# Gated channel mixing: the end of the kernel by batch pairs, its weights by way of DRAM, its gates without GpSimd

## The chip, the cores and the metric

One core of one Trainium2 chip runs the whole program. The metric is the device time of one execution in microseconds; a kernel's number is the median over its runs. A profile is one execution taken by the hardware profiler; in it TensorE is PE, VectorE is DVE, ScalarE is ACT, GpSimd is POOL and SyncE, which issues the DMAs, is SP.

## The reference

All tensors are float32, with 4 batches (B), 12 heads of 64, 448 positions (S) and 768 channels (D); the weights come as float64.

```
scores = q k^T / sqrt(64) - log(S);  x = sigmoid(scores) v        # heads joined: (4, 448, 768)
u = x + (x^T U V)^T                                              # U: 448 x 32, V: 32 x 448
y = u + relu(u w_ch1) w_ch2                                      # 768 -> 3072 -> 768
gate[:, s] = sigmoid(sum over k in 0..4 of conv_w[k] * y[:, s - 4 + k])     # per channel, zero ahead of s = 0
out = (gate * (y w_val)) w_out                                   # both weights 768 x 768
```

## The kernel before, in words

Channels lie on the 128 partitions, positions along the free dimension: `xs` holds x, then u, y and at last z = gate times value, as 6 channel blocks by 4 batches, each with four zeros ahead of its 448 positions (`x_of(b, m)` is one 128x448 block of it without the zeros). Every product with a weight is made of three passes of reduced precision (`mm3`, lines 175 to 177): high part by high part, high by low, low by high. So each operand is a pair of tiles, a rounded high part (ACT) and the rest, its low part (a subtraction). Operands lie in a pool of 32 slots (`operand`).

A weight comes in halves of 128x384 numbers as float64 bits (`load_half`, on SP's queue, three halves ahead) and is unpacked by four operations (`unpack`, lines 83 to 88), rounded by ACT (line 73) and subtracted by DVE (line 75) into a buffer of the pool `w` (`prep_half`). What `later=True` or `deferred` marks is put back until the next `flush`, which `product` and `ch2` call first, so that an engine's in-order queue does not wait there.

Stages, in the order in which the code is written (it is the order on each engine's queue; there is no other scheduler):

1. Attention by pairs of heads, woven with the mixing by U and V and the splitting of u. The first weights are unpacked beside it.
2. Twelve channel groups. A group has two chunks of 128 hidden channels: for each chunk and batch one `ch1` product (18 matmuls, relu and its low part), then for each batch and channel block one `ch2` (12 matmuls) whose result DVE adds to `xs`. Beside them stand 8 calls of `prep_half` a group, for the next group's weights.
3. In the last group every `ch2` is followed by `y_split`: high part on ACT, low part on POOL.
4. 24 value products `val(b, m)`, block by block over all four batches, with the value weights unpacked beside them; each is multiplied by its gate into z (line 432). The gate of a block takes five taps (`gate_steps`): three scalings on ACT (line 404), two additions on POOL (lines 410 and 414), two fused multiply-adds on DVE (line 417), a sigmoid on ACT (line 426). `before(i)` and `after(i)` spread these steps over the products around the i-th.
5. `z_split` for z of the first two batches beside the last four value products, of the others at the first two output products (lines 73 and 77).
6. 24 output products `fin` (block by block, all batches), each copied by ACT (line 441) and stored by SP (lines 619 and 621), with the output weights unpacked beside them.

Products go round through eight PSUM banks (`bank`).

Of the kernel before, what the change touches and what calls it, by code (L numbers as in the profile page):

```python
# [8 lines left out]
F32 = mybir.dt.float32  # L9
# [20 lines left out]
HQ = DM // 2  # L30
NP = B * H // 2
OPS = 32
WS = 5
LAG = 2
EARLY = 3

# [2 lines left out]
def tile_kernel(  # L39
# [82 lines left out]
    sources += [wval_in[m] for m in range(KC)] + [wout_in[m] for m in range(KC)]  # L122
    pools = {}
    wraw = {}
    wt = {}
    ready = set()
    at = {"load": 0, "prep": 0}

    def load_half():
        i = at["load"]  # L130
        if i >= 2 * len(sources):
            return
        n, half = divmod(i, 2)
        if i < EARLY:
            r = scratch(f"raw{i}")[:, :2 * HQ].bitcast(I64)
        else:
            r = pools["raw"].tile([P, HQ], I64, tag="raw", name=f"raw{i}")[:, :]
        nc.sync.dma_start(r, sources[n][:, half * HQ:(half + 1) * HQ])
        wraw[i] = words(r)
        at["load"] += 1  # L140

    def prep_half():
        i = at["prep"]
        if i >= 2 * len(sources):
            return
        flush()
        n, half = divmod(i, 2)
        if i < EARLY:
# [7 lines left out]
        wt.setdefault(n, []).append(t)  # L156
        unpack(wraw.pop(i), a, x)

        def high():
            split(f32(x), t[:, 0], t[:, 1], later=True)  # L160
            deferred.append(lambda: ready.add(i))

        deferred.append(high)
        at["prep"] += 1
# [3 lines left out]
    def weight(n):  # L168
        while not {2 * n, 2 * n + 1} <= ready:
            flush()  # L170
        return wt[n]

    def mm3(ps, w, k, x, start, stop):
        wk = w[k // 3][:, :, (k % 3) * P:(k % 3 + 1) * P]
# [205 lines left out]
    def ch2(g, b, m):  # L380
# [5 lines left out]
        y = x_of(b, m)  # L386
        nc.vector.tensor_add(y, ps[:, :S], y)  # L387

    def y_split(b, m):
        y = x_of(b, m)  # L390
        t = operand(f"y{b}_{m}")
        nc.scalar.activation(t[:, 0], y, AF.Copy)  # L392
        nc.gpsimd.tensor_sub(t[:, 1], y, f32(t[:, 0]))  # L393
        ys[b, m] = t

    def gate_steps(b, m):

        t = []
        y = xs[:, m, b]
        z = x_of(b, m)  # L400
        tap = lambda k: f32(cw[:, m * TAPS + k:m * TAPS + k + 1])

        def scaled(dst, k):
            nc.scalar.activation(dst, y[:, k:k + S], AF.Copy, scale=tap(k))

        def first():
            t.append(operand(f"g{b}_{m}", F32))
            scaled(t[0][:, 0], 0)
            scaled(t[0][:, 1], 1)
            nc.gpsimd.tensor_add(t[0][:, 0], t[0][:, 0], t[0][:, 1])  # L410

        def second():
            scaled(t[0][:, 1], 2)
            nc.gpsimd.tensor_add(t[0][:, 0], t[0][:, 0], t[0][:, 1])  # L414

        def fused(dst, k):
            nc.vector.scalar_tensor_tensor(
                dst, y[:, k:k + S], tap(k), t[0][:, 0], op0=ALU.mult, op1=ALU.add
            )

        return (
            first,
            second,
            lambda: fused(t[0][:, 0], 3),
            lambda: fused(z, 4),
            lambda: nc.scalar.activation(z, z, AF.Sigmoid),
        )

    def val(w, b, m):
        ps = product(f"val{b}_{m}", w, lambda k: ys[b, k])  # L430
        z = x_of(b, m)
        nc.vector.tensor_mul(z, ps, z)

    def z_split(b, m):
        t = operand(f"z{b}_{m}")
        split(x_of(b, m), t[:, 0], t[:, 1])
        zs[b, m] = t

    def fin(w, b, m, o):
# [83 lines left out]
    def main_phase(tail):  # L523
# [27 lines left out]
        ch1(0, B - 1)  # L551
        ch1(1, B - 1)

        todo = [(b, m) for m in range(KC) for b in range(B)]
        gates = [gate_steps(b, m) for b, m in todo]

        def gate(i, k):
            if 0 <= i < len(gates):
                gates[i][k]()

        def before(i):
            gate(i, 4)
            gate(i + 1, 2)

        def after(i):
            gate(i + 1, 3)
            gate(i + 2, 1)
            gate(i + 3, 0)

        for g in range(NG):  # L570
            n = 2 * G * g
            last = g == NG - 1
            if g == 0:
                flush()
            if g:
                for i in range(G):
                    for b in range(B):
                        ch1(g * G + i, b)
                        if i * B + b < 6:
                            prep_half()  # L580
                    wt.pop(n + i)
            for b in range(B):
                for m in range(KC):
                    ch2(g, b, m)
                    if last:
                        y_split(b, m)
                        if b == B - 1 and m in (2, 3, 4):
                            i = m - 5
                            before(i)
                            after(i)  # L590
                if g == 0 or last or b % 2 == 0:
# [5 lines left out]
        for i, (b, m) in enumerate(todo):  # L597
            before(i)
            val(weight(n + m), b, m)
            after(i)  # L600
            if m < KC - 1 and b in (0, 2):
                prep_half()
            if m == KC - 1:
                for k in range(3):
                    z_split(b // 2, 3 * (b % 2) + k)
        n += KC
        for m in range(KC):
            for p in range(2):
                o = operand(f"o{p}_{m}", F32)
                for j in range(2):  # L610
                    b = 2 * p + j
                    fin(weight(n + m), b, m, o[:, j])
                    if m == 0 and b < 2:
                        for k in range(KC):
                            z_split(b + 2, k)
                    if b >= 2:
                        prep_half()
                    if m == KC - 1 and p == 1:
                        nc.sync.dma_start(out[m, :, b], o[:, j])
                if m < KC - 1 or p == 0:  # L620
                    nc.sync.dma_start(out[m, :, 2 * p:2 * p + 2], o)

    with tc.manual_schedule():
        mixc = pool(ctx, "mixc", 1)
# [11 lines left out]
        next(work)  # L636
        att.close()
        end = scope()
        pools["w"] = pool(end, "w", 2 * WS)
        banks.append(pool(end, "ps_m", 4, space=PSUM))  # L640
        for _ in work:
            pass
# [43 lines left out]
```

## Time and profile before

| | |
|---|---|
| median of 3 runs | 1093.49 us (1092.12 to 1095.51) |
| the profiled execution | 1092.42 us, of which the span from the first to the last instruction is 1090.6 us |
| busy, share of the span | PE 1060.4 us (97%), DVE 683.1 (63%), ACT 330.8 (30%), POOL 91.9 (8%) |
| granted PE clock, mean | 0.989 of full |
| DMA | 70.64 MB, mean 65 GB/s |

Busy times are those of the engine's instructions, laid over each other only once. A clock of 1.00 is 2.4 GHz and one of 0.50 is 1.2 GHz.

### The profile page before, as it was taken

To read this page: it belongs to the slowest core of one execution; us is meant where nothing else is said; L and a number is where in the kernel's file an instruction comes from. 1 tells how busy PE (TensorE), PEld (TensorE's weight loads), DVE (VectorE), ACT (ScalarE), POOL (GpSimd) and SP (SyncE) were. 2 spreads that over 40 slices of the span, in tenths; PEclk is the share of its full clock that TensorE was granted. 3 is DMA by queue.
4 is the path that set the end of the run, shared out by engine and by line. 5 is a ranking of instruction groups with operands and counts; after the bars stand their busy time and mean duration, and the time that the engine had idled before them with its cause. 6 is when DMAs were issued, how large, how long until landed. Compare 5 with 4: busy or idle time off the path is not lost.

```text
span 1090.6 us, 13524 instructions
## 1 busy us (share of the span) xinstructions
PE 1060.4 (97%) x5464; PEld 901.5 (83%) x5464; DVE 683.1 (63%) x1247; ACT 330.8 (30%) x565; POOL 91.9 (8%) x77
## 2 busy tenths in 40 slices
PE   8999999999999999999999999999999999975998
PEld 3444446899999999999999999999999999964997
DVE  4454657786666666666566666666656788889510
ACT  5677776302010111111010202020111345557221
POOL 0000000000000000000000000000000485553000
PEclk9999999999999999999999999999999999995999
DMA  6333332213121211212121313121212212110311
GB/s 164 102 103 86 92 104 84 64 53 102 29 73 29 74 44 58 59 44 73 29 73 29 87 29 87 29 73 29 73 44 58 59 30 58 45 44 19 122 68 68
DMA packets 28303, 70.64 MB, mean 65 GB/s; under 512 B 3520, under 2 KB 7216, under 8 KB 28240
## 3 DMA queue, kind: packets, MB, share of 16 engines
q1 hardware_dynamic: 28160, 69.66, 22.5%
q8 instruction: 43, 0.70, 0.3%
q14 instruction: 20, 0.16, 0.1%
q10 hardware_dynamic: 80, 0.11, 0.0%
HBM read 64.26 MB, written 5.51 MB: 64 GB/s over the span
## 4 chain that ended last, share of the span: by engine, by line
PE 88%; POOL 5%; issue 3%; DVE 2%; ACT 0%; DMA 0%; SPq 0%; POOLq 0%; ACTq 0%
PE ch L175 21%; PE ch L177 21%; PE ch L176 21%; PE av L250 7%; PE sc L229 6%; PE fin L176 3%; PE fin L177 3%; PE fin L175 3%; POOL g L414 2%; POOL g L410 2%; PE tr L309 1%; PE pp L323 1%; PE h L345 1%; POOL y L393 1%; DVE z L77 0%
## 5 line engine op out<-in xcount | busy, mean ns | idle before, releaser
L387 DVE TENSOR_TENSOR xs<-ch,xs 128x448 f32<-128x448 f32 x288 | 175.8, 622 | 101.8 <-PE ch L177 101.7
L73 ACT ACTIVATE w<-x 128x384 fp32r<-128x384 f32 x120 | 63.0, 525 | 499.9 <-DVE x L88 496.4
L175 PE MATMUL ch<-u,w 128*128 128x448 f32 x576 | 210.9, 366 | 0.0
L175 PE MATMUL ch<-h,w 128*128 128x448 f32 x576 | 210.6, 366 | 0.0
L176 PE MATMUL ch<-h,w 128*128 128x448 f32 x576 | 210.6, 366 | 0.0
L177 PE MATMUL ch<-h,w 128*128 128x448 f32 x576 | 210.5, 366 | 0.0
L176 PE MATMUL ch<-u,w 128*128 128x448 f32 x576 | 210.5, 365 | 0.0
L177 PE MATMUL ch<-u,w 128*128 128x448 f32 x576 | 210.5, 365 | 0.0
L375 DVE SCALAR_TENSOR_TENSOR h<-ch,h 128x448 fp32r<-128x448 f32 x96 | 59.9, 624 | 133.2 <-ACT h L374 133.2
L175 PEld LDWEIGHTS ch<-u,w 128*128 128x128 f32 x576 | 108.3, 188 | 9.7 <-issue 1.3
L177 PEld LDWEIGHTS ch<-h,w 128*128 128x128 f32 x576 | 108.3, 188 | 8.4
L177 PEld LDWEIGHTS ch<-u,w 128*128 128x128 f32 x576 | 108.3, 188 | 8.4
L175 PEld LDWEIGHTS ch<-h,w 128*128 128x128 f32 x576 | 108.3, 188 | 8.4
L176 PEld LDWEIGHTS ch<-h,w 128*128 128x128 f32 x576 | 108.3, 188 | 8.4
L176 PEld LDWEIGHTS ch<-u,w 128*128 128x128 f32 x576 | 108.4, 188 | 8.3
L393 POOL TENSOR_TENSOR y<-xs,y 128x448 fp32r<-128x448 f32 x24 | 29.0, 1223 | 863.8 <-ACT y L392 863.4
L237 ACT ACTIVATE a<-sc,bias 112x896 f32<-112x896 f32 x96 | 91.5, 1002 | 24.3 <-PE sc L229 23.9
L75 DVE TENSOR_TENSOR w<-x,w 128x384 fp32r<-128x384 f32 x120 | 67.2, 560 | 30.6 <-ACT w L73 29.0
L374 ACT ACTIVATE h<-ch 128x448 fp32r<-128x448 f32 x96 | 51.1, 533 | 109.4 <-PE ch L177 109.3
L250 PE MATMUL av<-a,vr 112*64 112x448 f32 x384 | 82.8, 552 | 0.0
L229 PE MATMUL sc<-ks 64*112 64x448 f32 x576 | 73.4, 387 | 5.1 <-ACT ks L214 5.1
L229 PEld LDWEIGHTS sc<-ks 64*112 64x112 f32 x576 | 48.0, 176 | 30.5 <-ACT a L237 9.4
(75 smaller groups left out, 1183.1 us busy)
## 6 DMA issues: line engine op xcount, KB each, us to landing
raw<-in_w SPq DMA_DIRECT2D x96, 384.0 KB, 3.1
kq<-in_kq SPq DMA_DIRECT2D x47, 224.0 KB, 3.8
vr<-in_va SPq DMA_DIRECT2D x24, 224.0 KB, 2.6
out_t<-o SPq DMA_DIRECT2D x11, 448.0 KB, 2.5
raw<-in_wval SPq DMA_DIRECT2D x12, 384.0 KB, 3.1
raw<-in_wout SPq DMA_DIRECT2D x12, 384.0 KB, 3.2
out_t<-o SPq DMA_DIRECT2D x2, 224.0 KB, 1.9
vraw<-in_v SPq DMA_DIRECT2D x3, 112.0 KB, 3.7
```

The lines of the kernel that those rows point to most:

```text
L73: nc.scalar.activation(hi, raw, AF.Copy)
L75: deferred.append(lambda: nc.vector.tensor_sub(lo, raw, f32(hi)))
L175: mm(ps, wk[:, 0], x[:, 0], start=start, stop=False)
L176: mm(ps, wk[:, 0], x[:, 1], start=False, stop=False)
L177: mm(ps, wk[:, 1], x[:, 0], start=False, stop=stop)
L229: mm(ps[:SC, h, :S], ks[r, tk, 0, c * SC:(c + 1) * SC], ks[r, tq, 1], start=t == 0, stop=t == 2,)
L237: nc.scalar.activation(a[:SC], ps[:SC, :, :S], AF.Sigmoid, bias=bias[:SC], scale=1.0 / math.sqrt(D))
L250: mm(ps[D * h:D * h + D, :S], vr[:, h, c], a[:SC, h], start=c == 0, stop=c == NSC - 1,)
L374: nc.scalar.activation(t[:, 0], ps, AF.Relu)
L375: nc.vector.scalar_tensor_tensor(t[:, 1], ps, 0.0, f32(t[:, 0]), op0=ALU.max, op1=ALU.subtract)
L387: nc.vector.tensor_add(y, ps[:, :S], y)
L393: nc.gpsimd.tensor_sub(t[:, 1], y, f32(t[:, 0]))
```

## The change

Value and output weights (24 halves, numbers 96 to 119) are unpacked inside the channel groups, in a written-out sequence `order` ("c" is a half of a channel group's weight, "s" one of these), at 10 or 11 `prep_half` a group. When such a half is done it is written to DRAM (`stash`) and its buffer is free again. In the end it is read back (`fetch`) once for each pair of batches, without unpacking. The pool `w` has 11 buffers where it had 10.

The last group and everything behind it run by pairs of batches: ch1 and ch2 of batches 0 and 1, then of 2 and 3; value products of the first pair, of the second; output products of the first pair, of the second. Gates are made for two batches in one operation of 128x896: one scaling on ACT, four fused multiply-adds on DVE, one sigmoid on ACT; two of the twelve beside the second pair's ch1, the others beside the value products. The low part of y is subtracted on DVE. z is split one block per product: the first pair's beside the second pair's value products, the second pair's beside the first pair's output products. One of `unpack`'s operations is ACT's instead of DVE's.

```diff
-WS = 5
+WS = 11
@@ unpack
-        nc.vector.tensor_scalar(a, f32(high), 2.0 ** -112, None, op0=ALU.mult)
+        nc.scalar.activation(a, f32(high), AF.Copy, scale=2.0 ** -112)
@@ the sequence of halves
+    plan("c" * 9 + "cccscs")
+    for g in range(1, NG - 1):
+        plan("ccccccss" + ("ccs" if g < 3 else "cc"))
+    plan("ccc")
@@ prep_half
+        def done(t):
+            ready.add(i)
+            if i >= 4 * NF:
+                stash[i] = pools["stash"].tile([P, 2, HQ], F32, tag="stash", name=f"s{i}")
+                nc.sync.dma_start(stash[i][:, :, :], f32(t))
+    def fetch(n, p):
+        fetched[n, p] = ts = []
+        for half in range(2):
+            t = pools["w"].tile([P, 2, HQ], F32R, tag="w", name=f"f{n}_{p}_{half}")[:, :, :]
+            nc.sync.dma_start(f32(t), stash[2 * n + half][:, :, :])
+            ts.append(t)
@@ y_split
-        nc.gpsimd.tensor_sub(t[:, 1], y, f32(t[:, 0]))
+        lows[b, m] = lambda: nc.vector.tensor_sub(t[:, 1], y, f32(t[:, 0]))
@@ gate_steps(bs, m), y(k) = xs[:, m, both batches, k:k + S]
+            nc.scalar.activation(t[0], y(0), AF.Copy, scale=tap(0))
+        def add(k):
+            nc.vector.scalar_tensor_tensor(
+                y(k) if k == PAD else t[0], y(k), tap(k), t[0], op0=ALU.mult, op1=ALU.add
+            )
@@ the value products
+        for v, (p, m, b) in enumerate(todo):
+            later.append((v // 2, val(fetched[n + m, p], b, m)))
+            settle_values(1)
+            gate_half()
+            y_low()
+            if p:
+                z_split(*unsplit.pop(0))
+            if v % 2:
+                fetch_next()
```

What this makes of DVE's queue in the middle of the value products. Before (val1_2 is the value product of batch 1 and block 2, g2_2 the gate of batch 2 and block 2, the last number is the program's):

```order
L417 SCALAR_TENSOR_TENSOR xs_61<-xs_61,cw_62,g1_2_7751 128x448
L83 TENSOR_SCALAR a107_7825<-raw107_7624 128x384
L84 TENSOR_SCALAR x107_7826<-raw107_7624 128x384
L85 SCALAR_TENSOR_TENSOR x107_7826<-a107_7825,x107_7826 128x384
L88 SCALAR_TENSOR_TENSOR x107_7826<-raw107_7624,x107_7826 128x384
L417 SCALAR_TENSOR_TENSOR g2_2_7790<-xs_61,cw_62,g2_2_7790 128x448
L432 TENSOR_TENSOR xs_61<-val1_2_7836,xs_61 128x448
L417 SCALAR_TENSOR_TENSOR xs_61<-xs_61,cw_62,g2_2_7790 128x448
L417 SCALAR_TENSOR_TENSOR g3_2_7820<-xs_61,cw_62,g3_2_7820 128x448
L75 TENSOR_TENSOR w107_7824<-x107_7826,w107_7824 128x384
```

Of the change, at two value products of the first pair (g2_0 is now the gate of batches 2 and 3 in block 0):

```order
L467 TENSOR_TENSOR xs_61<-val1_3_7931,xs_61 128x448
L447 SCALAR_TENSOR_TENSOR g2_0_7900<-xs_61,cw_62,g2_0_7900 128x896 x2
L427 TENSOR_TENSOR y3_2_7718<-xs_61,y3_2_7718 128x448
L467 TENSOR_TENSOR xs_61<-val0_4_7961,xs_61 128x448
L447 SCALAR_TENSOR_TENSOR g2_0_7900<-xs_61,cw_62,g2_0_7900 128x896
L447 SCALAR_TENSOR_TENSOR xs_61<-xs_61,cw_62,g2_0_7900 128x2x448
L427 TENSOR_TENSOR y3_3_7728<-xs_61,y3_3_7728 128x448
```

The unpacking is gone from here, the two fused steps of a block have become four of double length per pair, and a low part of y stands after each half gate; the multiplication by gate comes one product late.

DVE's queue at the turn to the output products, before (z0_3 is the split z of batch 0 and block 3):

```order
L417 SCALAR_TENSOR_TENSOR g3_5_8234<-xs_61,cw_62,g3_5_8234 128x448
L432 TENSOR_TENSOR xs_61<-val2_5_8283,xs_61 128x448
L417 SCALAR_TENSOR_TENSOR xs_61<-xs_61,cw_62,g3_5_8234 128x448
L77 TENSOR_TENSOR z1_0_8304<-xs_61,z1_0_8304 128x448
L77 TENSOR_TENSOR z1_1_8307<-xs_61,z1_1_8307 128x448
L77 TENSOR_TENSOR z1_2_8310<-xs_61,z1_2_8310 128x448
L432 TENSOR_TENSOR xs_61<-val3_5_8314,xs_61 128x448
L77 TENSOR_TENSOR z1_3_8334<-xs_61,z1_3_8334 128x448
```

And of the change:

```order
L467 TENSOR_TENSOR xs_61<-val3_3_8261,xs_61 128x448
L75 TENSOR_TENSOR z0_4_8311<-xs_61,z0_4_8311 128x448
L467 TENSOR_TENSOR xs_61<-val2_4_8291,xs_61 128x448
L75 TENSOR_TENSOR z1_4_8334<-xs_61,z1_4_8334 128x448
L467 TENSOR_TENSOR xs_61<-val3_4_8314,xs_61 128x448
L75 TENSOR_TENSOR z0_5_8361<-xs_61,z0_5_8361 128x448
L467 TENSOR_TENSOR xs_61<-val2_5_8341,xs_61 128x448
L75 TENSOR_TENSOR z1_5_8384<-xs_61,z1_5_8384 128x448
L467 TENSOR_TENSOR xs_61<-val3_5_8364,xs_61 128x448
L75 TENSOR_TENSOR z2_0_8413<-xs_61,z2_0_8413 128x448
```

The last gate steps have moved ahead of these rows, and the splits of z are spread, one by one, between the multiplications.

## Rows read from the trace of the kernel before

**Rows 1.** The summary page: span, busy time, and the granted clock in 40 slices.
```profile
span 1090.6 us, 13524 instructions
PE 1060.4 (97%) x5464; PEld 901.5 (83%) x5464; DVE 683.1 (63%) x1247; ACT 330.8 (30%) x565; POOL 91.9 (8%) x77
...
PEclk9999999999999999999999999999999999995999
```

**Rows 2.** Stretches: length, busy PE, PEld, DVE, ACT, POOL (instructions); clock, DMA share, GB/s.
```profile
350.00:880.00 530.00, 530.00 (x2616) 491.86 (x2616) 337.23 (x657) 82.10 (x163) 16.99 (x15) 1.00 0.20 55
884.87:974.37 89.50, 88.18 (x433) 80.78 (x431) 75.53 (x105) 50.64 (x91) 56.18 (x44) 1.00 0.16 45
974.37:993.35 18.98, 0.17 (x1) 0.00 (x0) 16.79 (x24) 11.25 (x22) 11.57 (x10) 0.64 0.14 42
993.35:1003.54 10.19, 8.74 (x21) 6.80 (x22) 10.19 (x17) 6.73 (x15) 2.22 (x2) 0.50 0.00 1
1003.54:1086.65 83.11, 83.11 (x412) 77.10 (x410) 24.15 (x52) 21.32 (x44) 0.00 (x0) 1.00 0.24 83
```

**Rows 3.** PE in order of time, from the last value matmul on: start, duration.
```profile
974.17 0.37 PE L177 MATMUL val<-y,w 128*128 128x448 f32 x1
993.35 0.74 PE L175 MATMUL fin<-z,w 128*128 128x448 f32 x1 [18.81 <-ACT z L73]
...
1003.54 0.38 PE L175 MATMUL fin<-z,w 128*128 128x448 f32 x1
...
1086.65 0.37 PE L177 MATMUL fin<-z,w 128*128 128x448 f32 x1
```

**Rows 4.** Waits from 884 to 994 us: total, times, longest.
```profile
POOL g L414 <- ACT g L404: 36.4, 20, 2.9
...
PE fin L175 <- ACT z L73: 18.8, 1, 18.8
```

**Rows 5.** The gates' tiles: duration ns least, median, most; first and last start.
```profile
L404 ACT ACTIVATE g<-xs,cw x72: 651/655/673, 887.8 to 994.6; 128x448 f32<-128x448 f32 x72
L410 POOL TENSOR_TENSOR g<-g x24: 1117/1220/1552, 889.6 to 992.9; 128x448 f32<-128x448 f32 x24
...
L417 DVE SCALAR_TENSOR_TENSOR g<-xs,cw,g x24: 674/682/1567, 893.1 to 1000.2; 128x448 f32<-128x448 f32 x24
L417 DVE SCALAR_TENSOR_TENSOR xs<-xs,cw,g x24: 670/680/1383, 894.7 to 1001.3; 128x448 f32<-128x448 f32 x24
```

**Rows 6.** DVE's groups from 884 to 1004 us: busy us, mean ns, idle before.
```profile
L417 DVE SCALAR_TENSOR_TENSOR g<-xs,cw,g 128x448 f32<-128x448 f32 x24 | 25.9, 1080 | 15.2 <-POOL g L414 15.2
L417 DVE SCALAR_TENSOR_TENSOR xs<-xs,cw,g 128x448 f32<-128x448 f32 x24 | 20.5, 856 | 0.1
L432 DVE TENSOR_TENSOR xs<-val,xs 128x448 f32<-128x448 f32 x24 | 14.7, 614 | 0.0
L83 DVE TENSOR_SCALAR a<-raw 128x384 f32<-128x384 f32 x11 | 13.8, 1255 | 0.0
```

**Rows 7.** DVE's unpacking, groups from 0 to 880 us.
```profile
L88 DVE SCALAR_TENSOR_TENSOR x<-raw,x 128x384 uint32<-128x384 uint32 x101 | 57.2, 567 | 3.5
L75 DVE TENSOR_TENSOR w<-x,w 128x384 fp32r<-128x384 f32 x101 | 55.7, 552 | 2.9 <-ACT w L73 1.4
...
L83 DVE TENSOR_SCALAR a<-raw 128x384 f32<-128x384 f32 x99 | 36.8, 372 | 0.0
```

**Rows 8.** The one DVE operation with two inputs of 128x896, in attention.
```profile
L210 DVE TENSOR_TENSOR ks<-kq,ks x23: 1091/1092/1094, 8.8 to 167.0; 128x896 fp32r<-128x896 f32 x23
```

**Rows 9.** ACT's copies (line 73), and DVE in time at the z splits.
```profile
L73 ACT ACTIVATE w<-x x120: 514/525/529, 174.1 to 1054.7; 128x384 fp32r<-128x384 f32 x120
...
L73 ACT ACTIVATE z<-xs x24: 559/564/573, 992.7 to 1010.0; 128x448 fp32r<-128x448 f32 x24
...
1004.07 8.11 DVE L77 TENSOR_TENSOR z<-xs,z 128x448 fp32r<-128x448 f32 x15
```

**Rows 10.** DMA issues: count, KB each, median us to landing.
```profile
raw<-in_w SPq DMA_DIRECT2D x96, 384.0 KB, 3.1
```

More of the change, by code (lines that the diff above doesn't have):

```diff
@@ L125, in tile_kernel @@
     wt = {}
+    stash = {}
+    fetched = {}
     ready = set()
@@ L419, in fused, with rest @@
             )
+        def rest():
+            y_low(*[(b, m) for b in bs])
+            add(3)
+            add(4)
         return (
             first,
[L423 to L426, printed above, removed]
+            lambda: (add(1), add(2)),
+            rest,
+            lambda: nc.scalar.activation(y(PAD), y(PAD), AF.Sigmoid),
         )
     def val(w, b, m):
+        y_low(*[(b, k) for k in range(KC)])
@@ L552, in main_phase @@
         ch1(1, B - 1)
[L554 to L570, printed above, removed]
+        for g in range(NG - 1):
             n = 2 * G * g
-            last = g == NG - 1
             if g == 0:
@@ L584, in main_phase @@
                     ch2(g, b, m)
[L585 to L591, printed above, removed]
+                    if m == KC // 2 - 1 and b % 2 and g == 0:
+                        prep_half()
+                if g == 0 or b % 2 == 0 or (b == 1 and g < 3):
                     prep_half()
@@ L594, in main_phase @@
                 wt.pop(n + G + i)
-        n = 2 * G * NG
[L597 to L605, printed above, removed]
+        halves = [range(h, h + B // 2) for h in range(0, B, B // 2)]
+        gates = [gate_steps(bs, m) for bs in halves for m in range(KC)]
@@ new lines, in main_phase, with gate_half @@
+        open_at = [0]
+        finished = []
+        def gate_half():
+            i, k = divmod(open_at[0], 2)
+            if i >= len(gates):
+                return
+            open_at[0] += 1
+            gates[i][1 + k]()
+            if k:
+                if i + 2 < len(gates):
+                    gates[i + 2][0]()
+                deferred.append(lambda: (gates[i][3](), finished.append(i)))
+        n = 2 * G * NG
+        g = NG - 1
+        fetches = [(n + q * KC + m, p) for q in range(2) for p in range(2) for m in range(KC)]
@@ new lines, in fetch_next @@
+        def fetch_next():
+            if fetches:
+                fetch(*fetches.pop(0))
+        for p, bs in enumerate(halves):
+            for i in range(G):
+                for b in bs:
+                    ch1(g * G + i, b)
+                    if p == 0:
+                        prep_half()
+                    else:
+                        y_low()
+                        y_low()
+                        gate_half()
+            if p:
+                for _ in range(3):
+                    fetch_next()
+            for b in bs:
+                for m in range(KC):
+                    ch2(g, b, m)
+                    y_split(b, m)
+                    if p == 0 and m % 2:
+                        y_low()
+            if p == 0:
+                flush(every=True)
+                gates[0][0]()
+                gates[1][0]()
@@ L606, in main_phase @@
         n += KC
-        for m in range(KC):
-            for p in range(2):
+        for p, bs in enumerate(halves):
+            for m in range(KC):
                 o = operand(f"o{p}_{m}", F32)
[L610 to L618, printed above, removed]
+                end = p and m == KC - 1
+                for j, b in enumerate(bs):
+                    fin(fetched[n + m, p], b, m, o[:, j])
+                    settle_values(0)
+                    if unsplit:
+                        z_split(*unsplit.pop(0))
+                    if end:
```

69 lines of the change are left out of this document (41 added, 28 removed).

## The prediction

> **What bounds the kernel now.** I read the summary first: TensorE (PE) is busy 97% of a span of 1090.6 us, and the granted clock is below full in one slice only, close to the end [rows 1]. So everything that is not PE at its pace is to be looked for there. The table by stretches then shows the middle of the program (350 to 880 us): PE busy all the time at full clock [rows 2]. In the stretch of the 432 matmuls of the value products it is busy 88.18 of 89.50 us; then comes a stretch of 18.98 us in which PE does nothing; then 10.19 us at half clock (1.2 instead of 2.4 GHz), for 21 matmuls; and from 1003.54 us on full clock again, without a gap [rows 2].
>
> The pace of PE when nothing holds it: from 1003.54 to 1086.65 us there are 410 steps from one matmul's start to the next one's (432 output matmuls less the first 21 and less one), so 83.11/410 = 0.2027 us a step [rows 2, 3]. One product of 18 matmuls is 3.65 us, a value stage or an output stage of 24 products 87.57 us.
>
> Why PE stands still: its longest wait, 18.8 us, is that of the first output matmul for the high half of z on ScalarE (ACT) [rows 4]. z is gate times value, and the gates were late. The list of waits says where they were made: GpSimd (POOL) waits for ACT's scaled taps and the others for POOL in turn [rows 4], the first of POOL's two additions per gate alone takes 1.2 us, the second goes the same way [rows 5], and the 24 gates stretch from 887.8 us (the first scaled tap) to 1001.3 (the start of the last step on VectorE) [rows 5]: 4.7 us per gate against 3.65 us per value product. PE runs ahead until the PSUM banks are full (PE then loses 1.9 us inside the stage), and at the turn to the output stage all that lag is paid at once, with the clock on top: it is at half rate after the standstill.
>
> **The change, part by part.**
>
> *What can be won.* The three losses, each against the pace of 0.2027 us: value stage 974.37 - 884.87 - 87.57 = 1.93 us (974.37 is the last value matmul's start, 974.17, and a step); standstill 993.35 - 974.37 = 18.98 us; half clock 10.19 - 21 x 0.2027 = 5.93 us [rows 2, 3]. Sum 26.84 us. PE has the same matmuls before and after, so this is the most that the end can give, and what is left to ask is whether the new order feeds PE without a wait.
>
> *Gating on VectorE (DVE).* Per channel block and batch pair there are now one ACT scaling, four fused multiply-adds of 128x896 on DVE and one sigmoid on ACT, 12 times. The trace has no fused operation of that length. Undisturbed, the 128x448 one takes 0.67 us (its minimum; the median is 0.68) [rows 5]. A two-operand instruction goes from 0.614 us at 448 columns [rows 6] to 1.092 us at 896 [rows 8], so 0.48 us for 448 more. I take 0.67 + 0.48 = 1.15 us. Bounds: below, 1.09 us, the row of 896 itself; above, twice the mean that the fused operations had beside POOL, 2 x (1.080 + 0.856)/2 = 1.94 us [rows 6].
>
> *Is DVE fast enough?* Two value products are 7.30 us of PE. In that time DVE has one gate (4 x 1.15 = 4.60), two multiplications of value by gate (2 x 0.614) [rows 6] and two low halves, of y in the first pair's products, of z in the second's (at most 2 x 0.614; fifteen of them in a row took 8.11 us, 0.54 each [rows 9]). That is 7.06 us, or 97%. Tight, but two of the twelve gates are made earlier, beside the second pair's ch1 products, the other ten beside the first twenty value products; the last four products have no gate and leave 4 x (3.65 - 1.23) = 9.7 us for catching up. DVE falls behind the end of the stage only if a fused operation takes over 1.15 + (10 x 0.24 + 9.7)/40 = 1.45 us.
>
> The 1.15 us hang on what slowed DVE before. The row: the same multiplication of 128x384 took 372 ns on average before 880 us [rows 7] and 1255 ns in the stretch in which POOL works [rows 6]. The Trainium skill, page "SBUF — State Buffer", section "Who interferes with whom", says that VectorE and GpSimd share one pair of SBUF ports, and that a VectorE instruction in a two-port mode or with two SBUF inputs and a GpSimd instruction block each other. By that rule the fused operation without POOL takes its undisturbed time and the sum is the one below; without it the 1.94 us stay and the time is that of the second rival. The trace agrees so far as it goes: the fused operations' minimum of 670 ns stands beside maxima of 1383 and 1567 [rows 5].
>
> *ACT in that stage.* Per two products a scaling and a sigmoid of 896, and two copies of 0.56 us [rows 9]. From 384 to 448 columns such a copy goes from 525 to 564 ns [rows 9], so 448 more are worth some 0.27 us, and at most a whole scaling of 448 once more, 0.66 us [rows 5]. The four sum to 2.9 us, at most 3.7, of 7.30. Not a bound.
>
> *The turn to the outputs.* Before, z was split after the last value products, three blocks at a time in front of the queue. Now the first pair's twelve z splits stand beside the second pair's value products, and the second pair's beside the first pair's output products: when the first output matmul comes up, all of its z but the last ones are done for many microseconds. I charge nothing; the cover is the second pair's 12 products (43.8 us). The same holds for y: the first pair's y is split during its ch2 and the second pair's ch1, the second pair's ch2 (144 matmuls, 29 us, in which DVE has 12 additions of the length of a multiplication by gate) follows before anybody needs it.
>
> *Channel groups: 24 unpackings of a half weight come into them*, one after each of the 8 ch1 products and two or three in ch2. One of the four unpacking operations goes from DVE to ACT. A half costs DVE 0.372 for the multiplication that stays, twice 0.567 and 0.552, 2.06 us instead of 2.43 [rows 7], and ACT 0.525 twice (an estimate for the scaling from the copy of the same shape [rows 9]). With the relu's low half a ch1 product takes 2.7 of 3.65 us of DVE and 1.6 of ACT. PE has eight banks of results in hand there. I charge 0; if the cover were gone, each would cost PE about the added ACT operation, 24 x 0.525 = 12 us. Before the groups, in the attention part, ACT gets six operations of at most 0.58 us among sigmoids with which PE never waits for it; below 3 us, I take 0.
>
> *DRAM.* 24 writes and 48 reads of 384 KB on SP's queue. A load of that size took 3.1 us from issue to landing [rows 10], so a weight of two halves 6.2 us even if one followed the other, and one is asked for per 7.30 us. Three weights are fetched before the value stage starts, during the second pair's ch2; each next one waits on SP only for a buffer whose last reader is several products back. What stands behind a fetch in SP's queue is the next fetch and, in the output stage, the output stores, which nobody waits for until the end. DMA engines were busy 24% at 83 GB/s in the output stage [rows 2]; two halves per 7.30 us are 108 GB/s, in place of the loads there, which keeps it below half. Charge 0. The queue also holds 24 stores that wait for a low half on DVE, with the next raw load behind them; the raw loads are three halves ahead, 11 us in ch1, against a landing of 3.1 us.
>
> *The end* (last copy, last stores) is the same: 0.
>
> **Sum.** Span 1090.6 - 26.84 = 1063.8 us; around the span there are 1092.42 - 1090.6 = 1.8 us, so 1065.6 us for the profiled execution. The median of the runs, 1093.49, is 1.07 us above that execution, so 1093.49 - 26.84 = 1066.65. I put 0.35 us on it for new hand-overs and forecast **1067 us**, 2.4% less. A change of 0.3% (3.3 us) is about what a measurement of this kernel can tell from none.
>
> **Rivals.**
>
> 1. *Part of the wait stays at the turn* (chance 0.09). DVE at 97% may run late by some microseconds, if a fused operation is not 1.15 but, say, 1.57 us (40 x 0.12 = 5 us over what the slack takes), or if the in-order queues wait for each other as long. Then the first output matmul waits 5 us, and the half clock comes back as it did after the standstill, another 5.9 us [rows 2]: 1066.65 + 10.9 = 1078 us. For it: only 0.24 us are free in 7.30. Against it: 9.7 us of slack in the last four products, and the z splits that are spread over twelve products.
>
> 2. *DVE is the new bound* (0.03). If the fused operation really takes 1.94 us, a gate is 7.76 us, and each of ten gates runs 7.76 + 2.46 - 7.30 = 2.9 us over. 29 us less 9.7 us of slack leave a standstill of 19 us, and with the half clock 25 us: 1066.65 + 25 = 1092 us, no change. Against it: the undisturbed rows.
>
> 3. *The groups wait* (0.05): the unpacking chain DMA, ACT, DVE, ACT, DVE is now longer and more frequent, and the relu stands behind it on ACT. Up to 12 us: 1079 us. Against it: PE never waits in the groups now, with six of eight ch1 products carrying such a chain.
>
> 4. *Slower: the weights come late* (0.03). Every weight is now read twice, from DRAM that the kernel wrote, and PE waits for it directly. Each of the 24 weights fetched would have to take 26.84/24 = 1.12 us longer than PE's 7.30 us, so over 8.4 us for two halves, before the gain is gone; at 10 us it would be 24 x 2.7 = 65 us of waiting and 1132 us. For it: two transfers for each weight, and stores in the same queue. Against it: 3.1 us a half.
>
> That the change does not do what it says would be that POOL was not the cause of the standstill; then the gain would be missing as in rival 2, and it is counted there.
>
> **Numbers.** Dense PE (0.80): 1064 to 1070, centred on 1067. Rivals 1 and 3 (0.14) lie at 1070 to 1079. The range 1063.5 to 1077 takes the likeliest case with its scatter and most of these two, and leaves out what is at 1092 and above. Faster 0.94, same 0.02 (most of rival 2), slower 0.04.
>
> **What would show it.** Right: in the profile after, PE busy with no gap from the last group to the end, full clock in all slices, 24 value products in 87.6 us, the first output matmul 0.2 us behind the last value matmul; fused operations of 128x896 at 1.15 us; POOL without additions; fetches landing in about 3 us. Wrong: a wait of PE for ACT or DVE at the first output product (rival 1 or 2, told apart by the length of the fused operation), for a fetched tile (rival 4), or gaps before the last group (rival 3).

## The result, and the profile after

| | before | after |
|---|---|---|
| median of 4 runs each, on one chip | 1093.36 us (1092.12 to 1095.51) | 1065.72 us (1065.50 to 1066.75) |
| ratio after to before | | 0.9747, 95% interval 0.9730 to 0.9764 |
| span of the profiled execution | 1090.6 us | 1063.5 us |

The kernel is 2.5% faster. The forecast was 1067 us in a range of 1063.5 to 1077; the sum gave a span of 1063.8 us.

The summary page of the changed kernel: span, busy time of each engine, granted clock in 40 slices, and the chain that ended last.

```profile
span 1063.5 us, 13752 instructions
...
PE 1054.6 (99%) x5464; PEld 897.7 (84%) x5464; DVE 649.8 (61%) x1148; ACT 353.5 (33%) x616; POOL 0.4 (0%) x5
...
PEclk9999999999999999999999999999999999999999
...
PE 99%; DMA 0%; ACT 0%; SPq 0%; issue 0%; ACTq 0%
```

PE is busy 99% in place of 97%, the slow slice of the clock in [rows 1] is gone, and the chain that ended last is PE from end to end. The same by stretches of the value stage, its last four products, and the output stage (length, then busy PE, PEld, DVE, ACT, POOL, the clock, the DMA share and GB/s, as in [rows 2]):

```profile
884.70:957.00 72.30, 72.30 (x358) 67.02 (x357) 66.86 (x80) 20.55 (x27) 0.00 (x0) 1.00 0.36 110
957.00:972.00 15.00, 15.00 (x75) 13.90 (x74) 5.31 (x10) 2.82 (x5) 0.00 (x0) 1.00 0.26 78
972.00:1040.00 68.00, 68.00 (x337) 63.03 (x336) 8.14 (x13) 15.40 (x30) 0.00 (x0) 1.00 0.44 150
```

PE has no gap, where [rows 2] had 18.98 us without PE and 10.19 us at half clock. DVE is busy 66.86 of 72.30 us, 6.75 per two value products, and then has room. The turn to the outputs is in PE's order of time, which answers to [rows 3]:

```profile
972.00 0.36 PE L208 MATMUL val<-y,f 128*128 128x448 f32 x1
972.21 0.36 PE L206 MATMUL fin<-z,f 128*128 128x448 f32 x1
```

The first output matmul follows 0.21 us behind the last value matmul; before, it waited 18.8 us [rows 4]. The gates' tiles (duration ns least, median, most; first and last start), which answer to [rows 5]:

```profile
L447 DVE SCALAR_TENSOR_TENSOR g<-xs,cw,g x36: 1142/1144/1152, 861.5 to 954.7; 128x896 f32<-128x896 f32 x36
L444 ACT ACTIVATE g<-xs,cw x12: 1027/1030/1040, 856.8 to 936.6; 128x896 f32<-128x896 f32 x12
L447 DVE SCALAR_TENSOR_TENSOR xs<-xs,cw,g x12: 1151/1152/1153, 866.5 to 955.9; 128x896 f32<-128x896 f32 x12
```

The fused operations have medians of 1.144 and 1.152 us, and hardly any scatter. And one line of the list of waits from 884 us on, DVE's wait for PE at the multiplication of value by gate (total, times, longest):

```profile
DVE xs L467 <- PE val L208: 14.3, 24, 2.5
```

All 24 multiplications now wait for their product: the gates are ahead of PE, before they were behind.

So far everything went as written. Whether it went so for the reason that the prediction gives is another question, and the trace after can't answer it, since the change did several things at once.

### The profile page after: what moved, and what is told of

Same layout as the page of the kernel before. It is cut to its first block, busy times and chain, and to the rows that moved or that the text cites. A ratio compares the mean times of both kernels' runs of the same rounds, so it can differ in the third digit from the quotient of the medians.

```text
span 1063.5 us, 13752 instructions
## 1 busy us (share of the span) xinstructions
PE 1054.6 (99%) x5464; PEld 897.7 (84%) x5464; DVE 649.8 (61%) x1148; ACT 353.5 (33%) x616; POOL 0.4 (0%) x5
## 4 chain that ended last, share of the span: by engine, by line
PE 99%; DMA 0%; ACT 0%; SPq 0%; issue 0%; ACTq 0%
PE ch L206 22%; PE ch L208 22%; PE ch L207 22%; PE av L281 7%; PE sc L260 7%; PE fin L207 3%; PE val L208 3%; PE val L207 3%; PE fin L208 3%; PE val L206 3%; PE fin L206 3%; PE tr L340 1%; PE pp L354 1%; PE h L376 1%; DMA kq<-in_kq 0%; ACT ks L245 0%
## 5 line engine op out<-in xcount | busy, mean ns | idle before, releaser
L85 DVE SCALAR_TENSOR_TENSOR x<-a,x 128x384 uint32<-128x384 uint32 x117 | 65.5, 560 | 14.4 <-ACT a L83 2.1
L88 DVE SCALAR_TENSOR_TENSOR x<-raw,x 128x384 uint32<-128x384 uint32 x120 | 67.0, 558 | 4.2
```

The costliest lines, as they stand in the source:

```text
L85: nc.vector.scalar_tensor_tensor(x, a.bitcast(U32), 3, x, op0=ALU.logical_shift_left, op1=ALU.bitwise_or)
L88: nc.vector.scalar_tensor_tensor(x, high, 0x80000000, x, op0=ALU.bitwise_and, op1=ALU.bitwise_or)
```

## The experiments

**Theory A** is the prediction's: GpSimd's additions set the pace of the gates, 4.7 us each; taking them off GpSimd is the gain. **Theory B**: it was the unpacking of the weights that stood among the gates on DVE and ACT; moving it into the channel groups is the gain. **Rival C**: what counts is the new order by batch pairs, which has z ready at the turn. All ratios are to the kernel before on the same chip.

### Take the unpacking out of the end, and nothing else

The kernel before, with the value and output weights unpacked in the groups and kept in DRAM as in the change, each fetched once. Order, gates on GpSimd and all else stay.

```
-WS = 5
+WS = 11
...
                         ch1(g * G + i, b)
-                        if i * B + b < 6:
-                            prep_half()
+                        prep_half()
...
-            val(weight(n + m), b, m)
+            val(fetched[n + m], b, m)
...
-            if m < KC - 1 and b in (0, 2):
-                prep_half()
+            if b == B - 1:
+                fetch(n + m + 3)
...
-                    fin(weight(n + m), b, m, o[:, j])
+                    fin(fetched[n + m], b, m, o[:, j])
```

> Kernel before with one part of the change: value and output weights unpacked in the channel groups, kept in DRAM and fetched once each; old order of batches, old gates with GpSimd. Theory A (the prediction's: GpSimd's two additions per gate are the pace): the gates keep some 4.5 us each against 3.65 us of a value product, PE stands still again at the turn, 1085 to 1093 us. Theory B (the unpacking among the gates is the pace: in the trace of before ACT waits 11 times, 28 us in all, for the unpacking on DVE before it can round a weight, and the gates' scalings stand behind it in ACT's queue; the chain of waits has 2.9 us of it per two gates of 9.0 us): without it two gates take 6.1 us, less than two products, PE hardly waits, 1066 to 1071 us.

Measured: **1065.81 us** (1065.59 to 1066.85), ratio 0.9750 (0.9733 to 0.9766): the whole gain, with every addition still on GpSimd. Theory A, that this chain is the pace, falls. Nor is it that the weights are ready earlier: PE has no wait for a weight in the kernel before, from 860 us on. The trace shows what is at work. First its 45 us in the middle of the value stage (columns as above):

```profile
902.00:947.00 45.00, 45.00 (x224) 41.75 (x223) 45.00 (x41) 30.84 (x52) 34.82 (x27) 1.00 0.16 45
```

Then GpSimd's and DVE's operations on the gates' tiles:

```profile
L443 POOL TENSOR_TENSOR g<-g x24: 1152/1157/1543, 886.0 to 966.1; 128x448 f32<-128x448 f32 x24
L446 DVE SCALAR_TENSOR_TENSOR g<-xs,cw,g x24: 673/1574/1580, 887.2 to 971.0; 128x448 f32<-128x448 f32 x24
L446 DVE SCALAR_TENSOR_TENSOR xs<-xs,cw,g x24: 670/1480/1497, 889.2 to 972.2; 128x448 f32<-128x448 f32 x24
```

And one gate after another on DVE (start, duration):

```profile
931.27 0.61 DVE L461 TENSOR_TENSOR xs<-val,xs 128x448 f32<-128x448 f32 x1
931.80 1.49 DVE L446 SCALAR_TENSOR_TENSOR xs<-xs,cw,g 128x448 f32<-128x448 f32 x1
933.21 1.58 DVE L446 SCALAR_TENSOR_TENSOR g<-xs,cw,g 128x448 f32<-128x448 f32 x1
934.71 0.61 DVE L461 TENSOR_TENSOR xs<-val,xs 128x448 f32<-128x448 f32 x1
```

GpSimd slows DVE more than it did before: the fused operation's median is 1.57 and 1.48 us instead of 0.68. Yet from one multiplication (L461) to the next it is 3.44 us, less than the 3.65 of a value product, and from 897 to 962 us every step is as long; DVE is busy all the while, as the gates catch up with PE. GpSimd's chain can therefore deliver a gate in 3.44 us, and what it took before was not its own pace.

One GpSimd addition in the kernel before, and then all of DVE in one period of two gates:

```profile
920.05 1.19 POOL L414 TENSOR_TENSOR g<-g 128x448 f32<-128x448 f32 x1 [0.78 <-ACT g L404]
...
919.67 0.55 DVE L75 TENSOR_TENSOR w<-x,w 128x384 fp32r<-128x384 f32 x1
920.14 0.61 DVE L432 TENSOR_TENSOR xs<-val,xs 128x448 f32<-128x448 f32 x1
920.68 1.04 DVE L417 SCALAR_TENSOR_TENSOR xs<-xs,cw,g 128x448 f32<-128x448 f32 x1
921.65 1.31 DVE L83 TENSOR_SCALAR a<-raw 128x384 f32<-128x384 f32 x1
922.88 0.35 DVE L84 TENSOR_SCALAR x<-raw 128x384 uint32<-128x384 uint32 x1
923.26 0.56 DVE L85 SCALAR_TENSOR_TENSOR x<-a,x 128x384 uint32<-128x384 uint32 x1
923.86 0.56 DVE L88 SCALAR_TENSOR_TENSOR x<-raw,x 128x384 uint32<-128x384 uint32 x1
924.34 0.68 DVE L417 SCALAR_TENSOR_TENSOR g<-xs,cw,g 128x448 f32<-128x448 f32 x1
924.93 0.62 DVE L432 TENSOR_TENSOR xs<-val,xs 128x448 f32<-128x448 f32 x1
925.46 0.68 DVE L417 SCALAR_TENSOR_TENSOR xs<-xs,cw,g 128x448 f32<-128x448 f32 x1
927.19 1.56 DVE L417 SCALAR_TENSOR_TENSOR g<-xs,cw,g 128x448 f32<-128x448 f32 x1 [1.05 <-POOL g L414]
928.67 0.55 DVE L75 TENSOR_TENSOR w<-x,w 128x384 fp32r<-128x384 f32 x1
```

From one L75 to the next are 9.00 us for two gates, 4.50 each (the 4.7 of the prediction has the first gate's start in it). The five unpacking operations (L75, L83 to L88) last 3.33 us of it, and DVE waits for GpSimd 1.05 us a period. The stretch from 902 to 947 us, here of the kernel before, holds five such periods (columns as above):

```profile
902.00:947.00 45.00, 45.00 (x224) 41.74 (x223) 39.42 (x55) 24.95 (x46) 26.51 (x20) 1.00 0.18 51
```

DVE is busy 39.42 us of them, 7.88 a period, against 7.30 for two products. GpSimd has a share in this sum. Three operations of the period are longer than by themselves: L83 with 1.31 us and the fused ones at 920.68 and 927.19 with 1.04 and 1.56, against 0.37, 0.68 and 0.68 [rows 5, 7], together 2.18 us. Less these, an estimate, DVE would have 5.7 us a period, and the unpacking would fit. So it seems to take both, the unpacking in DVE's queue and GpSimd's blocking of DVE; this is argued from the rows, as no run removes the blocking without handing GpSimd's additions to DVE. What the run shows is that moving the unpacking is enough: 6.88 us for two gates with GpSimd still there.

### Take GpSimd out of the end, and nothing else

The kernel before, all four additions of a gate as fused operations on DVE, and the low half of y on DVE too.

```
-        nc.gpsimd.tensor_sub(t[:, 1], y, f32(t[:, 0]))
+        nc.vector.tensor_sub(t[:, 1], y, f32(t[:, 0]))
...
-            scaled(t[0][:, 1], 1)
-            nc.gpsimd.tensor_add(t[0][:, 0], t[0][:, 0], t[0][:, 1])
...
-            scaled(t[0][:, 1], 2)
-            nc.gpsimd.tensor_add(t[0][:, 0], t[0][:, 0], t[0][:, 1])
+            fused(t[0][:, 0], 1)
+            fused(t[0][:, 0], 2)
```

> Kernel before with one part of the change: no GpSimd, all four multiply-adds of a gate (one batch each) and the low part of y on DVE; old order, weights still unpacked beside the value products. Theory A: with GpSimd's chain gone the gates come in time, 1066 to 1072 us. Theory B: DVE now has per two products 8 x 0.68 for the gates, 2 x 0.61 for the multiplications and one unpacking of 2.43, 9.1 us against 7.30, so the pace stays near 4.5 us a gate and the time between 1085 and 1097 us.

Measured: **1098.66 us** (1098.31 to 1100.10), ratio 1.0049 (1.0034 to 1.0065): 0.5% slower. DVE's operations on the gates' tiles:

```profile
L415 DVE SCALAR_TENSOR_TENSOR g<-xs,cw,g x72: 672/681/689, 903.2 to 1006.3; 128x448 f32<-128x448 f32 x72
```

Two multiplications of value by gate, two gates apart:

```profile
930.44 0.62 DVE L430 TENSOR_TENSOR xs<-val,xs 128x448 f32<-128x448 f32 x1
...
938.84 0.62 DVE L430 TENSOR_TENSOR xs<-val,xs 128x448 f32<-128x448 f32 x1
```

PE's longest wait from 860 to 1000 us is still the one at the turn:

```profile
PE fin L175 <- ACT z L73: 11.1, 1, 11.1
```

The contention is gone, no fused operation is over 0.69 us, and the gates still come late: 8.40 us for two, against 7.30. DVE's own sum says why: four fused operations of 0.68, a multiplication of 0.61 and half an unpacking of 2.43 [rows 7] are 4.5 us per gate (4.20 as measured, since neighbouring records overlap a little) against 3.65. Still, 8.40 is less than the 9.00 of before, and the wait at the turn fell from 18.8 to 11.1 us; what PE lost instead are 7.8 us of waits ahead of 912 us, for ch2's sums and for y. The low half of y in DVE's queue has its part in these, as the next two runs show. A kernel with the gates on DVE, the low half of y on GpSimd and the unpacking in place was not run, so what the gates' exchange of engines alone is worth stays open.

### Both, in the old order

The two edits above together, one batch per operation, no pairs.

> Kernel before with both parts, weights through DRAM and no GpSimd, but batches in the old order, one batch per gate operation and z split in threes beside the last four value products. Per product DVE has 4 x 0.68 + 0.61 = 3.3 of 3.65 us. Theories A and B: 1066 to 1070 us. Rival C (the order by pairs is needed): in the last four products DVE gets 12 splits of 0.54 on top, 19.7 us of work for 14.6, so PE waits some 5 us at the turn and its clock may fall: 1071 to 1078 us.

Measured: **1076.00 us** (1073.32 to 1076.88), ratio 0.9836 (0.9817 to 0.9854). The loss is not at the turn, so rival C falls, as it did with the first run, in the old order too; most of it lies at the start of the value stage. The stretches first:

```profile
900.00:915.00 15.00, 12.26 (x51) 10.39 (x50) 14.07 (x24) 5.02 (x9) 0.00 (x0) 0.89 0.17 54
...
957.00:972.00 15.00, 15.00 (x74) 13.63 (x73) 13.39 (x22) 6.74 (x14) 0.00 (x0) 1.00 0.00 1
972.00:990.00 18.00, 18.00 (x89) 16.36 (x88) 15.94 (x30) 10.07 (x22) 0.00 (x0) 1.00 0.03 10
```

Then the waits from 860 to 916 us:

```profile
ACT y L421 <- DVE xs L416: 29.3, 22, 3.3
DVE y L422 <- ACT y L421: 14.9, 23, 0.7
...
PE val L204 <- ACT y L421: 2.7, 1, 2.7
```

In the last `ch2` DVE adds a block, waits 0.65 us for ACT's high half, and makes the low half; the next addition stands behind it in the queue. That loop, with the first gates in it, makes the last blocks of y late, and PE waits and falls to a lower clock (0.89 in that stretch). After 915 us PE has no gap.

To tell the two parts of that edit apart, only the gates on DVE, and the low half of y back on GpSimd:

```
-        nc.vector.tensor_sub(t[:, 1], y, f32(t[:, 0]))
+        nc.gpsimd.tensor_sub(t[:, 1], y, f32(t[:, 0]))
```

> Kernel before with weights through DRAM; gates without GpSimd, one batch per operation on DVE; the low part of y stays on GpSimd. What the run with both on DVE lost, it lost before 915 us, beside ch2 of the last group, where each low part of y stands in DVE's queue ahead of the next ch2's addition and waits for ACT. If that is the whole of its loss: 1065 to 1068 us here. If the gates on DVE cost too (3.4 of 3.65 us a product, and 12 splits at the turn): 1070 to 1077 us.

Measured: **1066.30 us** (1066.10 to 1066.53), ratio 0.9756 (0.9742 to 0.9771), the whole gain again. So the 9.7 us between the two medians (taken on two chips) come from putting the low half of y into DVE's queue. Not all of them are waits: in the profile with the low half on DVE, PE's matmuls of the output stage are also a little longer, at a granted clock of 1.00 in both. The first line is that kernel, the second the one with the low half on GpSimd (duration ns; first and last start):

```profile
L204 PE MATMUL fin<-z,f x144: 367/368/369, 980.6 to 1069.2; 128*128 128x448 f32 x144
...
L204 PE MATMUL fin<-z,f x144: 362/365/369, 973.4 to 1060.4; 128*128 128x448 f32 x144
```

That is 88.6 us from first to last in place of 87.0, and why is open. Neither the pairs nor operations on two batches are needed.

### Put GpSimd back into the changed kernel

The first two additions of each gate on GpSimd as 128x896, with the scalings on ACT that they need.

```
         def first():
-            nc.scalar.activation(t[0], y(0), AF.Copy, scale=tap(0))
+            t.append(operand(f"e{bs[0]}_{m}", F32))
+            scaled(t[0], 0)
+            scaled(t[1], 1)
+            nc.gpsimd.tensor_add(t[0], t[0], t[1])
...
-            lambda: (add(1), add(2)),
+            second,
```

> Changed kernel with GpSimd back in the gates: the first two additions of each gate for two batches on GpSimd after scalings on ACT, the other two taps on DVE as now. Theory B: two additions of about 2.4 us and two hand-overs of 0.75 are some 6.3 us per two products of 7.30, so nothing waits: 1065 to 1068 us. Theory A: GpSimd's chain, and DVE slowed beside it, are what cost the time before and cost it here too: 1072 to 1092 us.

Measured: **1071.10 us** (1068.90 to 1073.07), ratio 0.9794 (0.9775 to 0.9814): 5.3 us more than the kernel of the first experiment beside it on the same chip, between the two expectations. DVE's third tap has 1134/2735/3004 ns (least, median, most) beside GpSimd's 2.13 us additions. The largest wait of PE, of those from 862 to 900 us, is not for a gate:

```profile
ACT xs L470 <- DVE xs L457: 15.4, 3, 6.0
...
PE ch L206 <- ACT h L405: 2.0, 1, 2.0
```

ACT's sigmoid waits up to 6.0 us for the late gate, the relu of the second pair's `ch1` stands behind it in ACT's queue, and PE waits for that. In this order GpSimd does cost something; in the old order with the unpacking gone it cost nothing.

### What in the unpacking was it: ACT's queue or DVE's time?

In the kernel before, ACT waits for DVE in order to round a half weight, 35.0 us from 860 to 1000 us, with the gates' scalings queued behind. **Theory B1**: that wait in ACT's queue set the pace. **Theory B2**: DVE's time did. The edit puts ACT's rounding back by one more product, so that it finds its input ready.

```
-        deferred.append(high)
+        if i >= 4 * NF:
+            deferred.append(lambda: deferred.append(high))
+        else:
+            deferred.append(high)
```

> Kernel before, unpacking still beside the value products; only the rounding of a value or output half on ACT comes one product later in ACT's queue, when DVE has finished the half. Theory B1 (the pace was ACT's queue, standing still for the unpacking): the 2.9 us per two gates shrink to what is left of DVE's work, 7.9 us busy per two gates against 7.30 of two products, so the lag at the turn falls from 19 to some 5 to 8 us: 1074 to 1083 us. Theory B2 (it was DVE's time itself, with every instruction lengthened beside GpSimd): two gates stay near 9 us, 1089 to 1095 us. Theory A: no change either.

Measured: **1098.95 us** (1098.43 to 1100.49), ratio 1.0057 (1.0042 to 1.0072). ACT's same wait from 860 to 1000 us:

```profile
ACT w L73 <- DVE x L88: 1.3, 1, 1.3
```

And the 45 us in the middle of the value stage:

```profile
902.00:947.00 45.00, 45.00 (x220) 40.87 (x219) 44.45 (x54) 22.52 (x41) 25.97 (x20) 1.00 0.15 45
```

The edit did what it should at that place, and nothing is gained: the kernel is 0.6% slower, above both expectations. ACT's queue does not stand still less, either. Its wait has moved to the sigmoid, which waits for the last fused operation on DVE, 35.5 us where it was 8.0:

```profile
ACT xs L429 <- DVE xs L420: 35.5, 11, 3.5
```

DVE, busy 39.42 of these 45 us before, is now full. B1 falls. DVE's groups in these 45 us show where the freed time went (busy us, mean ns):

```profile
L420 DVE SCALAR_TENSOR_TENSOR g<-xs,cw,g 128x448 f32<-128x448 f32 x10 | 12.1, 1211 | 0.0
L88 DVE SCALAR_TENSOR_TENSOR x<-raw,x 128x384 uint32<-128x384 uint32 x6 | 7.6, 1259 | 0.2
L75 DVE TENSOR_TENSOR w<-x,w 128x384 fp32r<-128x384 f32 x5 | 7.5, 1509 | 0.0
```

The unpacking operations now meet GpSimd's additions and take 1.26 and 1.51 us instead of 0.57 and 0.55 [rows 7]. That is what B2 says of the limit: DVE's operations, stretched beside GpSimd, fill its time as soon as a wait is taken away. Two gates now take 9.44 us. PE's matmuls are also longer again in this profile, with a median of 368 ns in both stages, and that is part of the loss.

### How much room the changed kernel has on DVE

One, and in a second kernel two, unused fused operations of 128x896 more per gate:

```
-            lambda: (add(1), add(2)),
+            lambda: (add(1), add(2), idle()),
...
+        def idle():
+            nc.vector.scalar_tensor_tensor(
+                spare[0], y(1), tap(1), t[0], op0=ALU.mult, op1=ALU.add
+            )
```

> Changed kernel with one more fused multiply-add of 128x896 per gate on DVE, its result unused. DVE's work per two value products goes from 6.75 to 7.9 us against 7.30. By the prediction's slack (two gates made early, four last products without gates, 9.7 us): no wait of PE, 1065 to 1067 us. If there is no slack and each gate's excess of 0.6 us over ten gates reaches PE: 1070 to 1074 us.

> Changed kernel with two more unused fused multiply-adds of 128x896 per gate on DVE: 9.1 us per two products against 7.30, 1.8 us over for each of ten gates, 18 us, of which the slack takes about 10: PE waits some 8 us, with or without a fall of its clock, 1072 to 1081 us. With no slack: 1083 to 1090 us. If DVE was never near its limit: 1065 to 1068 us.

Measured: **1066.30 us** with one (1065.92 to 1069.04), ratio 0.9763 (0.9742 to 0.9783); **1073.85 us** with two (1072.20 to 1074.98), ratio 0.9824 (0.9807 to 0.9841). With one, DVE is busy 70.59 of 72.30 us in the value stage and PE has no gap. With two, PE is busy 68.76 of it, and its wait there is for a low half of y, which stands behind the gates on DVE:

```profile
PE val L207 <- DVE y L428: 3.5, 1, 3.5
```

### The parts of the change that remain

Four small edits to the changed kernel: gates one batch per operation instead of two; every fetch from DRAM made twice, and three times (the copies are not used); and the one unpacking operation that went to ACT back on DVE. The core of each in this order:

```
+            for j, b in enumerate(bs):
+                x = xs[:, m, b, k:k + S]
...
+            r = pools["raw"].tile([P, HQ], I64, tag="raw", name=f"again{n}_{p}_{half}")[:, :]
+            nc.sync.dma_start(
+                r.bitcast(F32), stash[2 * n + half][:, :, :].rearrange("p t s -> p (t s)")
+            )
...
-        nc.scalar.activation(a, f32(high), AF.Copy, scale=2.0 ** -112)
+        nc.vector.tensor_scalar(a, f32(high), 2.0 ** -112, None, op0=ALU.mult)
```

> Changed kernel, gates of one batch per operation: 24 scalings, 96 multiply-adds and 24 sigmoids of 128x448 in place of 12, 48 and 12 of 896, in the same places of the order. If two short operations cost DVE 2 x 0.68 for one of 1.15, DVE has 7.6 us per two products against 7.30, ten gates leave 3 us of lag, inside the slack that the run with one more operation per gate showed: 1065 to 1068 us. If the number of operations matters to PE: 1070 us and above.

> Changed kernel, each fetch of a half weight from DRAM made twice, the second into a buffer that nobody reads: 96 reads of 384 KB. The trace after has DMA engines busy 0.36 in the value stage and 0.50 in the output stage with stores; doubled fetches make 0.7 and 0.85. If the weights' transfers have the room that the prediction gave them: 1065 to 1068 us. If they are close to their limit (latency in SP's one queue): PE waits for fetched tiles, 1070 to 1100 us.

> Changed kernel, each fetch made three times (144 reads of 384 KB), two of them into buffers that nobody reads. By the busy shares of the trace after the value stage would need 1.06 to 1.1 of the DMA engines and the output stage 1.2, so a weight takes 7.7 to 8.8 us against 7.30; with the lead of some 20 us at the start PE waits for some of the 24: 1068 to 1085 us. If it stays at 1065 to 1067 us, the shares overstate what a transfer needs.

> Changed kernel with the moved unpacking operation back on DVE: 120 times 0.37 us more on DVE, 0.53 less on ACT. In the groups DVE then has 3.05 of 3.65 us per ch1 product. All theories: no change, 1064 to 1068 us; a loss above 1070 us would mean that the groups are close to a limit on DVE.

| | median us | ratio (interval) |
|---|---|---|
| one batch per operation | 1065.98 | 0.9755 (0.9740 to 0.9770) |
| each fetch twice | 1065.62 | 0.9752 (0.9738 to 0.9767) |
| each fetch three times | 1065.41 | 0.9750 (0.9733 to 0.9766) |
| that operation on DVE | 1066.15 | 0.9756 (0.9741 to 0.9770) |

None of them moves the time by what can be measured. The stretches of the kernel with three fetches:

```profile
884.70:957.00 72.30, 72.30 (x359) 66.99 (x358) 66.69 (x79) 20.71 (x27) 0.00 (x0) 1.00 0.94 335
972.00:1040.00 68.00, 68.00 (x337) 63.02 (x336) 8.13 (x13) 15.40 (x30) 0.00 (x0) 1.00 0.85 297
```

The landing of the fetches that it uses (count, KB each, median us from issue):

```profile
f<-s SPq DMA_DIRECT2D x48, 384.0 KB, 5.7
```

The DMA engines are at 0.94 and 0.85 of their time, a fetch lands after 5.7 us instead of 3.4, and PE still has no gap. By the share of one fetch they were expected at 1.06 to 1.1 in the value stage, so that share overstates what three need. That asking for three weights ahead is what covers the 5.7 us is likely, but no run asked for fewer.

## Why the forecast held, and where its reasoning did not

**What can be won: right.** The three losses were 26.84 us and the span became 27.1 us shorter. PE had the same matmuls and nothing else to give, so any version that feeds PE through the end lands here; the changed kernel, the old order without its unpacking, and that with its gates on DVE lie within 0.6 us of each other. This, not the cause, carried the number; in that respect the forecast was lucky.

**The cause: wrong.** The step that failed is "The list of waits says where they were made: GpSimd (POOL) waits for ACT's scaled taps and the others for POOL in turn", from which the prediction took that GpSimd's chain makes the gates late. With the chain untouched and the unpacking gone the gates come every 3.44 us and the gain is whole; with the chain gone and the unpacking in place two gates still take 8.40 us, and the kernel is 0.5% slower. What the runs showed in its place: an unpacking of 3.33 us stood on DVE among each two gates, which took 9.00 us with it, against 7.30 for two products, and 6.88 without it. So "that the change does not do what it says would be that POOL was not the cause of the standstill; then the gain would be missing" failed as well: POOL's chain was not the cause by itself, and the gain came, because the same change moved the unpacking. The prediction priced that move on the receiving side, in the groups, and never on the side that it left. What the prediction says of GpSimd slowing DVE is so in the rows, 2.18 of the 7.88 us that DVE is busy per two gates, and it has a part in the lag that no run measures by itself. How the 9.00 us divide between unpacking, GpSimd's blocking and the hand-overs between DVE, ACT and GpSimd is not settled: taking ACT's wait away alone made DVE full.

**DVE fast enough: right, with a little more room than thought.** Forecast 1.15 us for the fused operation and 7.06 of 7.30 us per two products; measured 1.144 to 1.152 and 6.75. The prediction put the point from which it would fail at 0.30 us more per fused operation, 1.2 us per gate. An extra 1.15 us per gate cost nothing that can be measured, and twice that 8.1 us, so the point lies between the two, as forecast.

**ACT: right.** 20.55 of 72.30 us, 2.1 per two products; forecast 2.9.

**The turn: right.** 0.21 us. But the old order with the unpacking moved has no gap there either, so the spreading of the z splits was not needed for it.

**Groups: right at 0** (bound 12 us); the operation moved to ACT does not matter on either engine.

**DRAM: right at 0.** Fetches land after 3.4 us (forecast about 3), and the DMA share stays below half, 0.36 and 0.44. The GB/s are 110 in the value stage (forecast 108) but 150 in the output stage, where the prediction's figure left out the output stores. Rival 4 is far off: three times the reads cost nothing.

**The 0.35 us for hand-overs** were not needed: 1065.72 against 1066.65 without them.

## What to carry to other kernels

Add up what every engine does per product in the stage that waits, the side work included, before believing the chain of waits: the chain names who released last, not who was loaded. Take the durations from that stage: DVE has 7.88 us per two products with them, too much for 7.30, and some 5.7 with the undisturbed ones. Here 3.33 us of unpacking stood in DVE's queue in each 9.00 us, and moving it to a stage with spare time was worth everything, while handing GpSimd's work to DVE shortened two gates only to 8.40 us and made the kernel slower. And an operation moved to another engine joins a queue: the low half of y cost 9.7 us on DVE in the old order, where each next addition stood behind its wait.

## What was not expected of the hardware

GpSimd can stretch DVE's operations by more than a factor of two without costing time, as in the first experiment. A 128x448 fused operation goes from 0.67 to 1.57 us, a 128x896 one from 1.14 to 2.74 us (median beside GpSimd's 2.13 us additions), while the multiplication L461, of equal shape but with its first input in PSUM, stays at 0.61 us. In the kernel before, the same multiplication (L432, at 920.14) lies wholly beside the GpSimd addition of 920.05 to 921.24 that is shown above and takes 0.61 us too, and the fused operation next to it, which begins beside the same addition, takes 1.04 in place of 0.68. The Trainium skill, page "SBUF — State Buffer", section "Who interferes with whom", says that a VectorE instruction with at most one SBUF input, outside the two-port modes, does not contend with GpSimd; the trace agrees, with those 0.61 us beside 1.04.

The DMA engines moved 335 GB/s at a share of 0.94 during the matmuls, and PE's rows show nothing of it: 72.30 of 72.30 us busy, as with a third of the reads.
